# Experts begun at the last batch's gates, with u products inside a pair and D's rows split at half the pace

## The chip, the cores and the metric

The kernel runs on one core of a Trainium2 chip. Five engines work side by side, each through its own instructions in order: TensorE (PE in the profile, PEld for its weight loads), VectorE (DVE), ScalarE (ACT), GpSimd (POOL) and SyncE (SP), which here only issues DMAs. ACT issues some DMAs too. An engine that waits for a semaphore holds up everything behind it in its own order. The metric is the time of one execution in microseconds (us); lower is better. The median of three runs before the change is 789.2 us (788.12 to 789.28).

## The reference

Two mixers of the same input x (2048 rows, 640 columns) are blended by a gate per row:

```python
x = A_x
g = _sigmoid((x * gate_w).sum(-1, keepdims=True))
a = _A_ref(x, A_dft_seq_re, A_dft_seq_im, A_dft_hid_re, A_dft_hid_im)
b = _B_ref(x, B_w_q, B_k1, B_k2, B_u, B_v)
return g * a + (1 - g) * b
```

A is a Fourier mixing written as matrix products: `a = x @ dft_hid_re.T`, `b = x @ dft_hid_im.T`, and then `dft_seq_re @ a - dft_seq_im @ b`.

B is a layer of 256 tiny experts with 32 heads per row:

```python
q = jnp.einsum("nd,dhc->nhc", xf, w_q)          # 32 heads x 256 per row
s1 = jnp.einsum("nhd,ed->nhe", q[..., :dk], k1) # 16 scores
s2 = jnp.einsum("nhd,ed->nhe", q[..., dk:], k2) # 16 scores
# the two best of s1, the two best of s2, the two best of their 4 sums
# top_e: expert numbers i1 * 16 + i2 (2 per head), g: softmax of their sums
act = _gelu(jnp.einsum("nd,nhkd->nhk", xf, u[top_e]))
out = jnp.einsum("nhk,nhk,nhkd->nd", g, act, v[top_e])
```

## The kernel before

**Numbers and products.** Most matrices are held as two parts of type fp32r, a high one (`h`, made by an ACT copy, line 122) and the rest (`l`, made by a subtraction on POOL or DVE, line 123). `split` makes both; `mm3` (lines 127 to 129) multiplies them in three matmuls: high by high, high by low, low by high. Almost all of PE's work runs through `mm3`, so the profile has one line for many different products and the tiles' names tell them apart.

**The frame: 128 pieces.** The sequence transform is cut into 128 pieces n (`seq_piece`), 16 to each of eight parts q (real or imaginary matrix, four column blocks of 512). A piece is five `mm3`, 15 matmuls of 512 columns, into PSUM banks 0 to 4. A piece's tile of the matrix is loaded five pieces ahead into `wf`, and split three pieces ahead into one of four slots of `WS`. At the end of a part, ACT copies the banks out (L220), DVE multiplies them by the row gate (`gate_piece`, L192, which needs the DMA `grow`), and ACT stores them (`store_piece`). All other work is hung between the pieces: `at(n, f)` runs f behind piece n, and calls hung at one n run in the order in which they were registered. Every engine takes its instructions in the order that this yields. A tile that takes over another's buffer waits until all that read the old tile are done, those issued later among them.

**Stage 1, pieces 0 to 30.** x is loaded and split (`X`). The query weights and the keys are folded into one matrix: for each of eight groups G, at b = 6 + 3G, 32 narrow matmuls (`w_part`, L320) make a tile `wp`, which ACT copies out (L325; `wp` has one buffer, and bank 5 or 6 is freed by it). Three pieces later it is transposed in five blocks of 128: first blocks 0 to 3, then, behind the next group's `w_part`, block 4 (`w_transposes`, L331). Both go through PSUM bank 7, which ACT (L333) and DVE (L334) empty. The last group's blocks are transposed at pieces 28 and 29. Beside this run the loads and splits of u (`split_u`, pieces 24 to 28) and the first x transposed (`load_xT`, `split_xT`, piece 27).

**Stage 2, pieces 31 to 63.** Rows come in 8 pairs of 128-row tiles, four pieces to a pair. `score_half(i, a)` makes half of the scores of tile i, 15 matmuls of 512 columns into bank 5 or 6 in turn, and ACT copies them out (L424). `u_pair(p)` makes all 256 products of u for the pair, 30 matmuls of 256 columns, a gelu on ACT (L541) and two stores. A pair's order behind its four pieces is: half, half, half, then half with `u_pair`, the next pair's `split_xT` and the load of the pair after that. `xh` and `xl` have one buffer each, taken anew by every pair. On DVE `topk` picks the two best of each list, `gates` the two best sums and their softmax (per batch of four tiles), and `rows` sends expert numbers and gates through transposing DMAs (L499) into `ROWS` (ACT, L504).

**The pump.** DVE's small steps (`topk`, `gates`, `rows`, `experts`) are generators in a queue, `Pump`. Each `mm3` calls `run_bg(0.68)`, which adds `share` times 0.68 us to a credit, and while the credit is positive the next step is issued and its price taken off. Steps issued directly (`gate_piece`, `make_sums`, `split_sums`, the part sums) take their price off the same credit. `rows` is spaced out by PE time instead. `drain` issues steps without credit until a condition holds.

**Stage 3, pieces 64 to 127.** `experts` builds two one-hot matrices for each of 32 chunks on DVE (`build`, L581 to L583, price 3.3), in one of four sets of `HOT`, and two chunks on PE 16 small matmuls each (`use`, L604, into bank 5 or 6), whose result DVE reduces into `cd` (`sums`, L590 and L592, price 1.4). Chunks 0 to 15 (g = 0) need the rows of batches 0 and 1, the others those of 2 and 3. Experts begin once all rows are in place. From piece 120 on (`ending`) only sets 0 and 1 are taken, one chunk at a time; at piece 124 sets 2 and 3 (in the tile `WP`) must be free, because the last stage's ring takes their place, and `bg.drain` sees to it. Beside this, D (the hidden transform) is loaded and split (`load_dd`, `split_dd`), sums of stored parts are made (`sum_parts`, pieces 98 to 109), and sums of D's blocks (`make_sums`, `split_sums`, pieces 114 to 123; L689 to L693).

**Stage 4.** 70 steps of the hidden transform and of the expert values follow, with the same rings, and raw tiles (`take`, `give`) into which SP loads what is to be split. The rest of the chunks is pumped here too.

Of the kernel before, what the change touches and what calls it, by code (L numbers as in the profile page):

```python
# [8 lines left out]
F32 = mybir.dt.float32  # L9
# [7 lines left out]
P = 128  # L17
S = 2048
D = 640
# [71 lines left out]
def gated_mix_kernel(ctx: ExitStack, tc: tile.TileContext, xT, xn, dreT, dimT, wsre, wsim, wq, kT, uT, vv, gw, out):  # L91
# [259 lines left out]
            for n in range(2):  # L351
                nc.sync.dma_start(xf[p][:, n], xT[2 * p + n])

    def split_xT(p):
        if p < NP:
            xs[p] = tuple(big.tile([P, 2, KD, P], F32R, name=t, tag=t) for t in ("xh", "xl"))
            f = xf.pop(p)
            for n in range(2):
                split(f[:, n], xs[p][0][:, n], xs[p][1][:, n], nc.gpsimd)
            load_xT(p + 1)  # L360

    for n in range(NT - 4):
        at(n, load_x, n + 4)
# [7 lines left out]
    for G in range(NG + 1):  # L371
        b = 6 + 3 * G - 2 * (G == NG)
        if G:
            at(b, w_transposes, G - 1, 0, 4)
        if G < NG:
            for m in range(4 * G, 4 * G + 4):
                at(b, w_part, m)
            for i, m in enumerate(range(4 * G + WQB, 4 * G + WQB + 4)):
                at(b + i // 2, load_wq, m)
        if G:  # L380
            at(b + (G == NG), w_transposes, G - 1, 4, KD)
    n = b + 2
    at(n - 8, load_xT, 0)
    for k in range(KD):
        at(n - 8 + k, load_u, k)
        at(n - 6 + k, split_u, k)
    at(n - 3, split_xT, 0)
    N0 = n + 1

    def gate():  # L390
# [20 lines left out]
    picked, rowed = set(), set()  # L411

    def score_half(i, a):
        xh, xl = (t[:, i % 2] for t in xs[i // 2])
        if a == 0:
            while i > 1 and i - 2 not in picked:
                bg.one()
            scs[i] = p2.tile([P, HH, E], F32, name="sc", bufs=2)
        ps = ps_s()
        c = slice(a * TC, (a + 1) * TC)  # L420
        for k in range(KD):
            mm3(ps, xh[:, k, :], xl[:, k, :], WH[:, k, c], WL[:, k, c], k == 0, k == KD - 1)
            run_bg(0.68)
        nc.scalar.activation(scs[i].rearrange("p h e -> p (h e)")[:, c], ps, AF.Copy)  # L424
        if a == 1:
            picks(i, scs.pop(i))

    def topk(i, sc):
# [6 lines left out]
        for s in range(2):  # L435
# [10 lines left out]
            if s == 0:  # L446
# [2 lines left out]
                nc.vector.scalar_tensor_tensor(sc, eq, FAR, sc, op0=OP.mult, op1=OP.add)  # L449
                yield 1.44  # L450

    def gates(b):
        mm, rr = stats.pop(b)
        t1a, t2a = mm[:, 0, :, :H], mm[:, 0, :, H:]
        t1b, t2b = mm[:, 1, :, :H], mm[:, 1, :, H:]
        c = p2.tile([P, 3, NB, H], F32, name="cc")
        nc.vector.tensor_add(c[:, 0], t1a, t2a)
        nc.vector.tensor_add(c[:, 1], t1a, t2b)
        nc.vector.tensor_add(c[:, 2], t1b, t2a)
        pk = p2.tile([P, NB, H], F16, name="pk")  # L460
        nc.vector.tensor_tensor(pk, c[:, 1], c[:, 2], op=OP.is_ge)
        nc.vector.tensor_tensor(c[:, 1], c[:, 1], c[:, 2], op=OP.max)
        nc.vector.tensor_sub(c[:, 1], c[:, 1], c[:, 0])
        nc.scalar.activation(c[:, 2], c[:, 1], AF.Exp)
        yield 1.2
        rp = p2.tile([P, 2, NB, 2, 2, H], F16, name="rp")
        r = rp[:, :, :, 0]
        nc.vector.tensor_copy(r[:, 0, :, 0], rr[:, 0, :, :H])
        nc.vector.tensor_copy(r[:, 1, :, 0], rr[:, 0, :, H:])
        d = p2.tile([P, 2, NB, H], F16, name="dp")  # L470
        nc.vector.tensor_sub(d[:, 0], rr[:, 0, :, :H], rr[:, 1, :, :H])
        nc.vector.tensor_sub(d[:, 1], rr[:, 1, :, H:], rr[:, 0, :, H:])
        nc.vector.tensor_mul(d, d, pk[:, None].to_broadcast([P, 2, NB, H]))
        nc.vector.tensor_add(r[:, 0, :, 1], d[:, 0], rr[:, 1, :, :H])
        nc.vector.tensor_add(r[:, 1, :, 1], d[:, 1], rr[:, 0, :, H:])
        for n in range(2):
            nc.vector.tensor_copy(rp[:, n, :, 1], r[:, n])
        yield 1.3

        nc.vector.tensor_scalar(c[:, 1], c[:, 2], 1.0, None, op0=OP.add)  # L480
        nc.vector.reciprocal(c[:, 0], c[:, 1])
        nc.vector.tensor_scalar(c[:, 0], c[:, 0], GSCALE, None, op0=OP.mult)
        nc.vector.tensor_mul(c[:, 1], c[:, 0], c[:, 2])
        g = c[:, :2].rearrange("p k i h -> p i k h")
        gs = p2.tile([P, NB, 2, 2, H], F16, name="gs")
        nc.vector.tensor_copy(gs[:, :, 0], g)
        nc.vector.tensor_sub(gs[:, :, 1], g, gs[:, :, 0])
        gated[b] = (rp, gs)
        yield 1.5

    def rows(b):
        rp, gs = gated.pop(b)

        def load_rows(a):

            t = p2.tile([P, 3, P], F16, name="rt", bufs=2)
            for n in range(3):
                f = rp[:, n, a] if n < 2 else gs[:, a]
                nc.sync.dma_start(t[:, n, :], f.rearrange("p a k h -> p (a k h)"), transpose=True)  # L499
            return t  # L500

        def put_rows(a, t):
            i = b * NB + a
            nc.scalar.activation(ROWS[i // 8][:, :, :, i % 8], t, AF.Copy)  # L504
            rowed.add(i)

        got = {}

        def step(a):
            if a < NB:  # L510
                got[a] = load_rows(a)
            if a:
                put_rows(a - 1, got.pop(a - 1))

        for a in range(NB + 1):
            bg.space(lambda a=a: step(a), 5.0 if a else 16.0 if b == NT // NB - 1 else 8.0)
        yield 0.0
# [12 lines left out]
            bg.add(rows(NT // NB - 1))  # L530

    def u_pair(p):
        xh, xl = xs.pop(p)
        ps = ps_s((P, 2, 2 * P))
        for n in range(2):
            c = slice(n * P, (n + 1) * P)
            for k in range(KD):
                mm3(ps[:, n, :], UH[:, k, c], UL[:, k, c], xh[:, :, k, :], xl[:, :, k, :], k == 0, k == KD - 1)
            run_bg(1.8)
        act = p2.tile([P, 2, 2 * P], F32, name="act", bufs=2)  # L540
        nc.scalar.activation(act, ps, AF.Gelu_apprx_tanh)  # L541
        for n in range(2):
            nc.scalar.dma_start(actd[n][:, 2 * p * P:2 * (p + 1) * P], act[:, n])

    for p in range(NP):
        n = N0 + 4 * p
        for a in range(4):
            at(n + 1 + a, score_half, 2 * p + a // 2, a % 2)
        at(n + 4, u_pair, p)
        at(n + 4, split_xT, p + 1)  # L550
    N1 = N0 + 4 * NP + 1


# [12 lines left out]
    def experts():  # L566
# [7 lines left out]
        def build(g, c, s):  # L574
            pt, qt = (HOT[s // 2][:, s % 2, n].rearrange("p (m e t) -> p m e t", e=E, t=4) for n in range(2))

            def row(n):
                r = ROWS[g][:, n, 8 * c:8 * c + 8, :].rearrange("p b (s t) -> p (b s) t", t=4)
                return r[:, :, None, :].to_broadcast(shp)

            nc.vector.tensor_tensor(pt, row(0), wt, op=OP.is_equal)  # L581
            nc.vector.tensor_tensor(qt, row(1), wt, op=OP.is_equal)
            nc.vector.tensor_tensor(pt, pt, row(2), op=OP.mult)  # L583
# [28 lines left out]
        while todo or prev:  # L612
            group = []
            if todo:
                def few():
                    return len([s for s in free_sets if s < 2 or not ending]) < min(len(todo), 1 if ending else 2)
                if few():
                    yield from use(prev)
                    prev = []
                for n in range(min(len(todo), 1 if ending else 2)):  # L620
# [13 lines left out]
    def load_dd(m):  # L634

        if m < KD:
            draw[m] = big.tile([P, 2, D], F32, name="draw", tag=("xf", "xh", "xl")[m % 3])
            for a in range(2):
                w, k = divmod(2 * m + a, KD)
                nc.sync.dma_start(draw[m][:, a], (dreT, dimT)[w][k])  # L640
# [7 lines left out]
        if a == 1:  # L648
            draw.pop(m)

    for m in range(3):
        at(N1 + m, load_dd, m)
    for m in range(KD):
        for a in range(2):
            at(N1 + 3 + 2 * m + a, split_dd, m, a)
        at(N1 + 4 + 2 * m, load_dd, m + 3)

# [66 lines left out]
    at(NPC + 28, store_gates, 1)  # L726


    raw_free, raw_tags = deque(), [("wf", 1)] * 5 + [(f"X{s}", 2) for s in range(10, 16)] + [("xf", 2)]
    raw, sp = {}, {}  # L730

    def take(key):
        if raw_tags:
            t, n = raw_tags.pop(0)
            if t == "wf":
                raw_free.append(big.tile([P, TC], F32, name="ra", tag=t, bufs=5))
            else:
                r = big.tile([P, 2, TC], F32, name="ra", tag=t)
                raw_free.extend(r[:, a] for a in range(2))
        raw[key] = f = raw_free.popleft()  # L740
        return f

    def give(key):
# [245 lines left out]
    prep_split = {NPC - 4: (0,), NPC - 3: (1,), NPC - 2: (2,), NPC - 1: (3, 4)}  # L989
    WP = None  # L990
    for n in range(N0, NPC):
        ending = n >= NPC - 8
        share = 0.95 if p3 is None or ending else 1.05
        seq_piece(n)
        follow(n)
        if n >= N1 and p3 is None and len(rowed) == NT and n % NT not in (NT - 2, NT - 1):
            p2_stack.close()
            p3 = ctx.enter_context(tc.tile_pool(name="p3", bufs=1, reuse_waits="tile"))
            pools.append(p3)
            HOT.append(p3.tile([P, 2, 2, 16 * E * 4], F16, name="hot0"))  # L1000
            HOT.append(p3.tile([P, 2, 2, 16 * E * 4], F16, name="hot1", tag="WP"))
            bg.add(experts(), late=True)
        if n == NPC - 4:
            bg.drain(lambda: {2, 3} <= set(free_sets))
            HOT.pop()
# [56 lines left out]
```

## Time and profile before

| what | value |
|---|---|
| median of three runs | 789.2 us |
| the profiled execution | 790.35 us, its span 788.5 us |
| PE busy | 772.8 us, 98% of the span |
| DVE busy | 553.7 us, 70% |
| POOL, ACT busy | 336.2 us (43%), 275.0 us (35%) |
| mean granted TensorE clock | 0.994 |
| pieces 15, 31, 47, 63 end near | 68, 142, 263, 386 us (first L220) |
| pieces 79, 95, 111, 127 end near | 447, 505, 562, 628 us |

The span runs from the first to the last instruction; the execution's time has what lies around it as well. A name like "PE b L129" is the engine, the tile that is written and the line. Where PE is busy at a granted clock of 1.00, another engine's idle time costs nothing. A wait is put down to the instruction that released it. In the timeline a row's figures are its start, its length, and in brackets the idle time of its engine before it, with the releaser.

### The profile page before, as it was taken

The numbers are of one execution on the slowest core, as the hardware profiler recorded it, in microseconds if no ns is written. First come the engines' busy times: TensorE is split into PE (matmuls) and PEld (weight loads), VectorE is DVE, ScalarE is ACT, GpSimd is POOL, SyncE is SP. The second block draws the span as 40 slices with busy tenths as digits, with TensorE's granted clock in tenths as the row PEclk, the third lists the DMA queues.
The fourth block names the chain that finished last, engine by engine and source line by source line (L and its number), as shares of the span: only waits on it lengthen the run. The fifth ranks groups of instructions, "written<-read, shape, count | busy, mean of one in ns | idle before, by whom it ended". The sixth has DMA issues, their size and how long they took to land.

```text
span 788.5 us, 10998 instructions
## 1 busy us (share of the span) xinstructions
PE 772.8 (98%) x4116; PEld 626.0 (79%) x4116; DVE 553.7 (70%) x660; ACT 275.0 (35%) x445; POOL 336.2 (43%) x233
## 2 busy tenths in 40 slices
PE   8999999999999999999999999999999899999997
PEld 6777767887888888878888888888888688888886
DVE  5741042287898999999895178799799948836651
ACT  4434223322323523523533711311324353334350
POOL 5423324314424233144149643353456473468270
PEclk9999999999999999999999999999999899999999
DMA  9876893502112242130355342568744695559421
GB/s 339 328 293 193 339 336 131 200 6 95 45 56 86 63 154 81 52 123 29 96 187 169 119 147 73 170 212 283 259 175 161 206 303 199 141 176 306 130 82 67
DMA packets 75508, 130.31 MB, mean 165 GB/s; under 512 B 17088, under 2 KB 24128, under 8 KB 75200
## 3 DMA queue, kind: packets, MB, share of 16 engines
q1 hardware_dynamic: 62704, 112.18, 42.8%
q10 hardware_dynamic: 12752, 17.45, 6.0%
q8 instruction: 32, 0.52, 0.3%
q14 instruction: 20, 0.16, 0.1%
HBM read 102.84 MB, written 25.17 MB: 162 GB/s over the span
## 4 chain that ended last, share of the span: by engine, by line
PE 76%; issue 9%; DVE 8%; DMA 3%; POOL 2%; SPq 1%; ACT 0%; DVEq 0%; ACTq 0%; POOLq 0%
PE b L127 24%; PE b L129 24%; PE b L128 24%; PE b L320 2%; POOL xl L123 2%; DMA xr<-in_xn 1%; PE b L604 1%; DVE hot L583 1%; DMA gd<-cd 1%; DMA pd<-ST 1%; DVE tmp L590 1%; DMA wf<-in_wsre 1%; DVE tf L691 1%; PE b L331 1%; DVE tf L692 1%
## 5 line engine op out<-in xcount | busy, mean ns | idle before, releaser
L123 POOL TENSOR_TENSOR WS<-wf,WS 128x512 fp32r<-128x512 f32 x127 | 190.6, 1506 | 283.4 <-ACT WS L122 283.3
L127 PE MATMUL b<-WS,X 128*128 128x512 f32 x635 | 251.3, 396 | 0.0
L128 PE MATMUL b<-WS,X 128*128 128x512 f32 x635 | 248.9, 392 | 0.7 <-POOL WS L123 0.7
L129 PE MATMUL b<-WS,X 128*128 128x512 f32 x635 | 248.7, 392 | 0.0
L128 PEld LDWEIGHTS b<-WS,X 128*128 128x128 f32 x635 | 120.3, 189 | 25.7 <-POOL WS L123 1.5
L127 PEld LDWEIGHTS b<-WS,X 128*128 128x128 f32 x635 | 120.5, 190 | 25.4 <-issue 0.5
L129 PEld LDWEIGHTS b<-WS,X 128*128 128x128 f32 x635 | 120.0, 189 | 25.3
L122 ACT ACTIVATE WS<-wf 128x512 fp32r<-128x512 f32 x128 | 79.7, 627 | 156.8 <-PE b L129 87.9
L129 PE MATMUL b<-WU,xl 128*128 128x512 f32 x160 | 63.1, 394 | 2.2 <-POOL xl L123 1.7
L123 POOL TENSOR_TENSOR xl<-xf,xh 128x640 fp32r<-128x640 f32 x16 | 32.1, 2031 | 73.9 <-ACT xh L122 73.9
L127 PE MATMUL b<-WU,xh 128*128 128x512 f32 x160 | 62.3, 390 | 0.0
L128 PE MATMUL b<-WU,xh 128*128 128x512 f32 x160 | 62.3, 389 | 0.0
L424 ACT ACTIVATE sc<-b 128x512 f32<-128x512 f32 x32 | 20.2, 630 | 114.3 <-PE b L129 114.3
L123 POOL TENSOR_TENSOR WS<-ra,WS 128x512 fp32r<-128x512 f32 x32 | 46.4, 1472 | 28.8 <-ACT WS L122 27.3
L192 DVE SCALAR_TENSOR_TENSOR ST<-ST,grow 128x512 f32<-128x512 f32 x40 | 34.6, 928 | 31.3 <-DMA grow<-gdr 31.3
L438 DVE TENSOR_REDUCE mm<-sc 128x64 f32<-128x1024 f32 x32 | 38.9, 1216 | 25.0 <-ACT sc L424 24.5
L334 DVE TENSOR_TENSOR WU<-b,WU 128x512 fp32r<-128x512 f32 (+1 forms) x16 | 7.9, 491 | 59.5 <-ACT WU L333 59.5
L440 DVE TENSOR_TENSOR eq<-sc,mm 128x1024 f16<-128x1024 f32 x32 | 43.4, 1356 | 1.1
L123 POOL TENSOR_TENSOR WP<-ra,WP 128x512 fp32r<-128x512 f32 x18 | 28.4, 1587 | 33.8 <-ACT WP L122 33.6
L590 DVE TENSOR_TENSOR tmp<-b,mask 128x512 f32<-128x512 f32 x32 | 22.0, 688 | 25.4 <-PE b L604 24.5
L444 DVE TENSOR_REDUCE rr<-eq 128x64 f16<-128x1024 f16 x32 | 39.0, 1220 | 1.1
L129 PEld LDWEIGHTS b<-WU,xl 128*128 128x128 f32 x160 | 30.0, 188 | 11.2 <-POOL xl L123 5.1
(148 smaller groups left out, 1248.1 us busy)
## 6 DMA issues: line engine op xcount, KB each, us to landing
wq<-in_wq SPq DMA_DIRECT2D x32, 640.0 KB, 6.7
wf<-in_wsre SPq DMA_DIRECT2D x64, 256.0 KB, 5.2
wf<-in_wsim SPq DMA_DIRECT2D x64, 256.0 KB, 3.8
ra<-pd SPq DMA_DIRECT2D x50, 256.0 KB, 3.6
pd<-ST ACTq DMA_DIRECT2D x40, 256.0 KB, 3.9
xr<-in_xn SPq DMA_DIRECT2D x16, 320.0 KB, 5.9
xf<-in_xT SPq DMA_DIRECT2D x16, 320.0 KB, 3.3
ra<-pqs SPq DMA_DIRECT2D x20, 256.0 KB, 4.7
```

The lines of the kernel that those rows point to most:

```text
L122: nc.scalar.activation(h, f, AF.Copy)
L123: eng.tensor_sub(l, f, h.bitcast(F32))
L127: nc.tensor.matmul(o, wh, ah, start=first, stop=False, skip_group_check=more)
L128: nc.tensor.matmul(o, wh, al, start=False, stop=False, skip_group_check=more)
L129: nc.tensor.matmul(o, wl, ah, start=False, stop=last, skip_group_check=more)
L192: nc.vector.scalar_tensor_tensor(f, f, -1.0 if w else 1.0, g, op0=OP.mult, op1=OP.mult)
L320: nc.tensor.matmul(ps[32 * j:32 * j + 32, :HALF], kp[:, 8 * G // H, r, :], w[:, j], start=(r == 0), stop=(r == 1))
L424: nc.scalar.activation(scs[i].rearrange("p h e -> p (h e)")[:, c], ps, AF.Copy)
L438: nc.vector.tensor_reduce(m, sc, op=OP.max, axis=AX.X)
L440: nc.vector.tensor_tensor(eq, sc, m[:, :, None].to_broadcast([P, HH, E]), op=OP.is_equal)
L444: nc.vector.tensor_reduce(r, eq, op=OP.max, axis=AX.X)
L590: nc.vector.tensor_tensor(tmp, t.rearrange("p m (e t) -> p (m e) t", t=4), mask4[:, None, :].to_broadcast([P, 8 * E, 4]), op=OP.mult)
```

## The change

Five things are changed.

1. In stage 1 block 4 of each group is transposed one piece later than before, at b + 1 (the last group's stays where it was).
2. In stage 2 `xh` and `xl` are one tile each for the whole stage, and each half of a pair is split by a call of its own: `u_pair` stands ahead of the third score half, the next pair's first half is split right behind it, and the second half behind the fourth score half. The load of the pair after that is issued two pieces later.
3. `experts` are added as soon as the last batch's gates are made, with 10.0 taken from the credit. The last batch's rows and gates live in a tile of their own (`lb`, in the place of `xl`), so that the memory of stage 2 can be given up before the rows are sent. `share` stays 0.95 throughout. `ending` starts at piece 117, and while it lasts, chunks in sets 2 and 3 are used before another is built.
4. D's ten rows are split every second piece instead of every piece, through two buffers instead of three.
5. `take` hands out raw tiles that were never used before it hands out returned ones.

```diff
-    def split_xT(p):
+    def split_xT(p, n):
         if p < NP:
-            xs[p] = tuple(big.tile([P, 2, KD, P], F32R, name=t, tag=t) for t in ("xh", "xl"))
-            f = xf.pop(p)
-            for n in range(2):
-                split(f[:, n], xs[p][0][:, n], xs[p][1][:, n], nc.gpsimd)
-            load_xT(p + 1)
+            if not xs:
+                xs.update((t, big.tile([P, 2, KD, P], F32R, name=t, tag=t)) for t in ("xh", "xl"))
+            split(xf[p][:, n], xs["xh"][:, n], xs["xl"][:, n], nc.gpsimd)
...
-            at(b + (G == NG), w_transposes, G - 1, 4, KD)
+            at(b + 1, w_transposes, G - 1, 4, KD)
...
-    at(n - 3, split_xT, 0)
+    for a in range(2):
+        at(n - 3, split_xT, 0, a)
+    at(n - 2, load_xT, 1)
...
-        rp = p2.tile([P, 2, NB, 2, 2, H], F16, name="rp")
+        if b == NT // NB - 1:
+            f = last_rows()
+            rp = f[:, :8 * P].rearrange("p (n i a k h) -> p n i a k h", n=2, i=NB, a=2, k=2)
+            gs = f[:, 8 * P:12 * P].rearrange("p (i a k h) -> p i a k h", i=NB, a=2, k=2)
+        else:
+            rp = p2.tile([P, 2, NB, 2, 2, H], F16, name="rp")
+            gs = p2.tile([P, NB, 2, 2, H], F16, name="gs")
...
     for p in range(NP):
         n = N0 + 4 * p
         for a in range(4):
+            if a == 2:
+                at(n + 3, u_pair, p)
+                at(n + 3, split_xT, p + 1, 0)
             at(n + 1 + a, score_half, 2 * p + a // 2, a % 2)
-        at(n + 4, u_pair, p)
-        at(n + 4, split_xT, p + 1)
+        at(n + 4, split_xT, p + 1, 1)
+        at(n + 6, load_xT, p + 2)
...
-                if few():
+                if few() or ending and any(s > 1 for g, c, s in prev):
                     yield from use(prev)
                     prev = []
...
-            draw[m] = big.tile([P, 2, D], F32, name="draw", tag=("xf", "xh", "xl")[m % 3])
+            draw[m] = big.tile([P, 2, D], F32, name="draw", tag=("xf", "xh")[m % 2])
...
-            at(N1 + 3 + 2 * m + a, split_dd, m, a)
-        at(N1 + 4 + 2 * m, load_dd, m + 3)
+            at(N1 + 3 + 4 * m + 2 * a, split_dd, m, a)
+        at(N1 + 7 + 4 * m, load_dd, m + 2)
...
-        if raw_tags:
+        if not fresh and raw_tags:
             t, n = raw_tags.pop(0)
             if t == "wf":
-                raw_free.append(big.tile([P, TC], F32, name="ra", tag=t, bufs=5))
+                fresh.append(big.tile([P, TC], F32, name="ra", tag=t, bufs=5))
             else:
                 r = big.tile([P, 2, TC], F32, name="ra", tag=t)
-                raw_free.extend(r[:, a] for a in range(2))
-        raw[key] = f = raw_free.popleft()
+                fresh.extend(r[:, a] for a in range(2))
+        raw[key] = f = (fresh or raw_free).popleft()
...
-        ending = n >= NPC - 8
-        share = 0.95 if p3 is None or ending else 1.05
+        ending = n >= NPC - 11
         seq_piece(n)
         follow(n)
-        if n >= N1 and p3 is None and len(rowed) == NT and n % NT not in (NT - 2, NT - 1):
+        if n >= N1 and p3 is None and NT // NB - 1 in gated:
             p2_stack.close()
...
             bg.add(experts(), late=True)
+            bg.credit -= 10.0
```

More of the change, by code (lines that the diff above doesn't have):

```diff
@@ L413, in score_half @@
     def score_half(i, a):
-        xh, xl = (t[:, i % 2] for t in xs[i // 2])
+        xh, xl = (xs[t][:, i % 2] for t in ("xh", "xl"))
         if a == 0:
@@ L450, in topk, with last_rows @@
                 yield 1.44
+    LB = []
+    def last_rows():
+        if not LB:
+            LB.append(big.tile([P, 18 * P], F16, name="lb", tag="xl"))
+        return LB[0]
     def gates(b):
@@ L484, in gates @@
         g = c[:, :2].rearrange("p k i h -> p i k h")
-        gs = p2.tile([P, NB, 2, 2, H], F16, name="gs")
         nc.vector.tensor_copy(gs[:, :, 0], g)
@@ L491, in rows @@
     def rows(b):
-        rp, gs = gated.pop(b)
+        rp, gs = gated[b]
         def load_rows(a):
-            t = p2.tile([P, 3, P], F16, name="rt", bufs=2)
+            if b == NT // NB - 1:
+                t = last_rows()[:, (12 + 3 * (a % 2)) * P:][:, :3 * P].rearrange("p (n m) -> p n m", n=3)
+            else:
+                t = p2.tile([P, 3, P], F16, name="rt", bufs=2)
             for n in range(3):
@@ L532, in u_pair @@
     def u_pair(p):
-        xh, xl = xs.pop(p)
+        xh, xl = xs["xh"], xs["xl"]
         ps = ps_s((P, 2, 2 * P))
@@ L579, in row @@
                 return r[:, :, None, :].to_broadcast(shp)
+            assert rowed >= set(range(8 * g, 8 * g + 8))
             nc.vector.tensor_tensor(pt, row(0), wt, op=OP.is_equal)
@@ L649, in split_dd @@
             draw.pop(m)
-    for m in range(3):
+    for m in range(2):
         at(N1 + m, load_dd, m)
@@ L726, in gated_mix_kernel @@
     at(NPC + 28, store_gates, 1)
-    raw_free, raw_tags = deque(), [("wf", 1)] * 5 + [(f"X{s}", 2) for s in range(10, 16)] + [("xf", 2)]
+    fresh, raw_free, raw_tags = deque(), deque(), [("wf", 1)] * 5 + [(f"X{s}", 2) for s in range(10, 16)] + [("xf", 2)]
     raw, sp = {}, {}
     def take(key):
-        if raw_tags:
+        if not fresh and raw_tags:
             t, n = raw_tags.pop(0)
             if t == "wf":
-                raw_free.append(big.tile([P, TC], F32, name="ra", tag=t, bufs=5))
+                fresh.append(big.tile([P, TC], F32, name="ra", tag=t, bufs=5))
             else:
                 r = big.tile([P, 2, TC], F32, name="ra", tag=t)
-                raw_free.extend(r[:, a] for a in range(2))
-        raw[key] = f = raw_free.popleft()
+                fresh.extend(r[:, a] for a in range(2))
+        raw[key] = f = (fresh or raw_free).popleft()
         return f
```

## The prediction

> **What bounds the kernel now.** The table of engines comes first:
>
> ```profile
> PE 772.8 (98%) x4116; PEld 626.0 (79%) x4116; DVE 553.7 (70%) x660; ACT 275.0 (35%) x445; POOL 336.2 (43%) x233
> ```
>
> TensorE is the bound, and the change takes no matmul away. Time can only come from moments in which PE stands still or runs at a lower granted clock. The windows show where (busy time per engine, mean granted clock, DMA share, GB/s):
>
> ```profile
> 108.00:124.00 16.00, 14.16 (x81) 10.35 (x80) 4.02 (x5) 3.70 (x10) 3.86 (x3) 0.89 0.93 329
> 124.00:138.00 14.00, 14.00 (x89) 10.49 (x88) 3.55 (x5) 5.66 (x12) 6.71 (x5) 1.00 0.20 63
> 424.00:450.00 26.00, 26.00 (x116) 21.52 (x116) 0.29 (x1) 15.18 (x19) 19.60 (x15) 1.00 0.44 139
> 540.00:600.00 60.00, 60.00 (x357) 49.07 (x352) 54.14 (x74) 17.26 (x34) 28.15 (x21) 1.00 0.64 220
> 600.00:626.00 26.00, 22.09 (x147) 17.43 (x147) 24.64 (x37) 8.46 (x19) 15.87 (x12) 0.87 0.52 166
> ```
>
> The table of waits (total, times, longest) names what ended the holes:
>
> ```profile
> ACT wp L325 <- PE b L331: 13.5, 7, 2.2
> PEld b L129 <- POOL xl L123: 5.1, 7, 1.3
> PE b L604 <- DVE tmp L590: 3.9, 2, 3.0
> PE b L331 <- DVE WU L334: 3.2, 3, 1.8
> ```
>
> Three kinds of hole, then: the fifth transpose of a W group waits for the split of the first four (L331), a score half waits for the low part of x (xl), and expert products wait for the sums of earlier ones (L604). Here they are in the timeline, the idle time in brackets:
>
> ```profile
> 46.10 0.33 PE L331 MATMUL b<-identf,wp 128*128 128x128 f32 x1 [0.22 <-DVE WU L334]
> 60.55 0.33 PE L331 MATMUL b<-identf,wp 128*128 128x128 f32 x1 [1.13 <-DVE WU L334]
> 115.35 0.33 PE L331 MATMUL b<-identf,wp 128*128 128x128 f32 x1 [1.84 <-DVE WU L334]
> 335.61 0.39 PE L127 MATMUL b<-WU,xh 128*128 128x512 f32 x1
> 335.83 0.39 PE L128 MATMUL b<-WU,xh 128*128 128x512 f32 x1
> 337.14 0.50 PE L129 MATMUL b<-WU,xl 128*128 128x512 f32 x1 [0.92 <-POOL xl L123]
> 610.16 0.69 PE L604 MATMUL b<-hot 128*64 128x64 f16 x32
> 615.47 0.64 PE L604 MATMUL b<-hot 128*64 128x64 f16 x16 [3.02 <-DVE tmp L590]
> 616.99 0.64 PE L604 MATMUL b<-hot 128*64 128x64 f16 x16 [0.88 <-DVE tmp L590]
> ```
>
> **Part 1, the fifth transpose one piece later (+4.95, then -5.5).** For groups G = 0 to 6 it used to follow the 32 products of W at piece b; now it follows piece b+1. Its wait for L334 then lies behind 15 matmuls, some 3.4 us at the 0.22 to 0.23 us between starts above, so the idle 0.22 + 1.13 + 1.84 = 3.19 us goes. The window 108:124 ran at a mean clock of 0.89, although 124:138 with the same kind of work ran at 1.00: 0.11 x 16 = 1.76 us, which I put down to the idle time at 115 just before. Gain 4.95 us.
>
> The same edit moves a second wait. ACT copies each new wp (L325) into the one buffer that the fifth transpose of the group before still reads; the 13.5 us in seven waits above are that. Now ACT stands at L325 for a whole piece more, and behind it in ACT's order wait the splits of the pieces (L122). For the copies of groups 1 to 6 there is room: the split held up is for piece b+4, two pieces or 6.8 us after ACT goes on. For those of group 7 (b = 27) there is none. The fifth transpose of group 6 and the four of group 7 both fall behind piece 28, back to back. The four need PSUM bank 7 (so L333 and L334 of the fifth) and the new wp (so L325). ACT's order from the release on is in the timeline of before:
>
> ```profile
> 130.22 0.33 PE L331 MATMUL b<-identf,wp 128*128 128x128 f32 x1
> 130.65 0.77 ACT L325 ACTIVATE wp<-b 128x320 f32<-128x320 f32 x2 [2.01 <-PE b L331]
> 131.30 0.28 ACT L333 ACTIVATE WU<-b 128x128 fp32r<-128x128 f32 x1
> 131.46 0.43 ACT L122 ACTIVATE WU<-uf 128x256 fp32r<-128x256 f32 x1
> 131.76 1.37 ACT L122 ACTIVATE xh<-xf 128x640 fp32r<-128x640 f32 x2
> 133.02 0.64 ACT L122 ACTIVATE WS<-wf 128x512 fp32r<-128x512 f32 x1
> 134.46 0.60 ACT L333 ACTIVATE WU<-b 128x512 fp32r<-128x512 f32 x1 [0.81 <-PE b L331]
> 131.62 0.29 DVE L334 TENSOR_TENSOR WU<-b,WU 128x128 fp32r<-128x128 f32 x1 [2.26 <-ACT WU L333]
> ```
>
> After the change L333 of the fifth comes behind the WS copy: 0.43 from transpose to L325, then 0.65, 0.30, 1.26 and 0.54 (its 0.64 less the 0.1 by which such rows overlap) from start to start, 3.2 us; 0.32 more to L334, 0.29 of its own, and PE goes on 3.8 us after the transpose instead of 0.1: a new hole of 3.7 us where before there was none. Bounds: 1.3 us if only L325 and L334 counted, 3.8 if everything does. After an idle 1.84 us the clock cost 1.76; I take as much here (bounds 0 and twice that, 3.5). Loss 5.5 us. Part 1 nets about -0.5.
>
> **Part 2, scores (+4.1).** Until now both halves of xh and xl were made after the u products, with one piece (3.4 us) to cover ACT and POOL. Now the u products come before the third score half, the first half is split right behind them and the second behind the fourth score half; each has two pieces and two score halves, some 13 us, before it is read. The row for 337.14 starts 1.31 us after its neighbour instead of 0.22. Over the seven such places the excess of start-to-start time, with the 0.11 of the matmul after, is 0.67 + 0.67 + 0.41 + 0.37 + 0.41 + 1.19 + 0.37 = 4.1 us, between PE's own idle and the 5.1 us that the weight loads waited. The counts stay: per pair 30 u matmuls, one gelu, two stores on ACT, two splits. The next pair's two loads move past two pieces' wf loads on SP, and still have a piece, a score half and the u products before their split. ACT waits behind the gelu as before. Nothing in this order is late next, unless xf itself is; I count 0 for that.
>
> **Part 3, experts from the last gates (+6.2).** The planner credits 5 x 0.68 us per piece. A chunk costs 3.3 + 1.4 = 4.7. Before, experts were added at piece 80 and earned 3.57 a piece (share 1.05); by my count of credits 24 chunks were built when the last stage's rule began at piece 120. At piece 124 chunks 22 and 23 (sets 2 and 3) were built and not multiplied, so the drain there forced four products with one after another's sums behind make_sums on DVE: the hole at 612. Now they are added at piece 69 or 70, pay 10.0 first, and earn 3.23. First build at piece 73, and between 73 and 116 there are 44 x 3.23 = 142, less 11.25 for three gate pieces, 15 for the part sums, 6 and 1 for two sums and a split: 109, or 23 chunks. From 117 on only one chunk at a time is begun, and a pair in sets 2 and 3 is used before anything is built. Pieces 117 to 121 earn 16, less 6 + 3, enough for the build under way and then that use at piece 122. The drain at 124 finds nothing to do.
>
> What goes is the idle 3.02 + 0.88, and the lower clock behind it: 0.13 x 26 = 3.4 us by the window's 0.87, of which the share 22.09/26 in which PE ran is 2.8. Together 6.7. In its place chunks 24 and 25 are multiplied at piece 124 and need the banks of 22 and 23, whose sums stand ahead of the last make_sums, but behind the one before. I charge 0.5 (bounds 0 and the old 3.9).
>
> What the early start costs lies under this:
>
> ```profile
> 422.89 1.41 DVE L487 TENSOR_TENSOR gs<-cc,gs 128x256 f16<-128x256 f32 x1
> 450.63 4.20 DVE L192 SCALAR_TENSOR_TENSOR ST<-ST,grow 128x512 f32<-128x512 f32 x5 [26.33 <-DMA grow<-gdr]
> L581 DVE TENSOR_TENSOR hot<-rows,wtab x32: 675/683/1773, 454.9 to 683.1; 128x1024 f16<-128x1024 f16 x32
> L582 DVE TENSOR_TENSOR hot<-rows,wtab x32: 675/684/1782, 456.4 to 683.9; 128x1024 f16<-128x1024 f16 x32
> ```
>
> DVE stood idle for 26 us there. A build of three such operations takes 2.0 to 5.3 us; some nine fit before piece 85, so 18 to 48 us on a free engine. The grow load for piece 80 may hold DVE a few us; no product waits for it before piece 84. Batch 3's rows now wait for the repaid credit, and end at piece 84 instead of 80; the first group that needs them is built from 96.
>
> **Part 4, D's rows at half the pace, two buffers; raw tiles (0).** Ten splits stay ten, on ACT and POOL. They moved no matmul before and are needed only at piece 128, 40 pieces on. POOL, 19.60 of 26 us busy in that window, gets room. Loads stay ten, each behind a release two pieces old. The raw tiles change only which buffer SP fills; PE had no hole after 626, so a gain there is hidden, and a late load would have to lose five steps first.
>
> **Sum.** 4.95 - 5.5 + 4.1 + 6.2 = 9.75 us, from a profiled time of 790.35 (its span 788.5 and 1.85 around it), which lies 1.15 above the median 789.2 of the runs. By the median: **779.5 us**.
>
> **Rivals.**
> *The stop at piece 28 costs nothing*: 779.5 - 5.5 = 774.0. It needs the framework to tie L325 to something earlier than the fifth transpose. Against it, L325 waited for L331 seven times.
> *The drain stays*: DVE or the credits are later than my count and sets 2 and 3 are still in use at 124. Then 789.2 + 0.5 - 4.1 = 785.6. For it: DVE is 54.14 of 60 us busy ahead of that place.
> *The half clock at 116 isn't the idle time's doing*: W's narrow products and the transposes, which stay, cause it. Then part 1 gains 3.2 and the time is 781.3. Against it: other groups with the same products kept 1.00, as 124:138 shows. [...]
> *Slower: builds too dear beside POOL.* If each build took 5.3 us as in the longest rows, a chunk with its sums would take DVE 6.7 us against the 4.95 us of PE time (4.7/0.95) at which chunks are issued: 1.75 behind per chunk. With 11 us of lead between build and product, PE pays from the seventh chunk; if it lasts for the first 16, 28 - 11 = 17 us, and 779.5 + 17 = 796.5. It decides once the operations average over 1.2 us. For it: POOL's D splits now run beside the first builds. Against it: medians of 0.68. [...]
>
> **How the numbers follow.** Forecast 0.55; stop free 0.12; drain stays 0.12; clock stays 0.08; slower 0.08; nothing of it arrives (789) 0.05. A difference under 0.2% (1.6 us) can't be told from none. Faster takes the first four, less a little of the drain case: 0.85; same 0.07; slower 0.08. The forecast's own range is 776 to 784 (hole at 28 from 1.3 to 7.2 with its clock, 0 to 3.9 at 124). To leave out no more than 2 in 10, I go up to the drain case and take in the lower edge: 775 to 786.5.
>
> **What would show it.** Right: no idle before the fifth transposes; one new PE idle of some 3.7 us before an L331 group near 129 to 133 us, released by DVE L334, with a granted clock under 1 behind it; no PE wait for xl; DVE building hot from about 420; no PE wait for tmp near 600 to 617, and the clock at 1.00 there. Wrong: PE waiting for hot or tmp between 430 and 600, for WS after a W group, or an L604 wait at 612 as before.

## The result and the profile after

The changed kernel takes 782.58 us (median of six, 782.25 to 783.25), the kernel before 788.14 us beside it (six, 786.66 to 789.28). The ratio is 0.993 (95% interval 0.9918 to 0.9943): 5.6 us faster. The direction and the range held; the forecast of 779.5 was 3.1 us too low, and 9.7 us of gain were promised, of which 5.6 came. One execution of the kernel before, beside e9 to e11, took 851.05 us at a granted clock of 0.851 instead of 0.994 to 0.998, and no comparison rests on it.

The profiled execution of after took 782.4 us. Its page, table of engines:

```profile
span 780.6 us, 11020 instructions
PE 769.4 (99%) x4116; PEld 624.5 (80%) x4116; DVE 564.5 (72%) x660; ACT 274.0 (35%) x445; POOL 333.7 (43%) x233
```

The same matmuls, and an end 7.9 us earlier than in the profile of before (that one was among the longer executions of its kernel, as will be seen). The windows of after, columns as before:

```profile
108.00:124.00 16.00, 16.00 (x105) 11.71 (x107) 5.63 (x9) 4.82 (x11) 4.82 (x4) 1.00 0.89 306
124.00:139.00 15.00, 11.52 (x64) 8.56 (x57) 2.80 (x6) 5.02 (x12) 5.71 (x4) 0.89 0.35 109
424.00:450.00 26.00, 26.00 (x173) 21.14 (x172) 23.21 (x23) 10.49 (x16) 16.07 (x11) 1.00 0.42 131
600.00:626.00 26.00, 26.00 (x186) 20.91 (x185) 23.14 (x34) 12.10 (x23) 14.25 (x12) 1.00 0.69 217
635.00:640.00 5.00, 4.08 (x17) 2.82 (x16) 0.00 (x0) 4.53 (x10) 4.51 (x4) 1.00 1.05 403
640.00:645.00 5.00, 4.39 (x34) 3.03 (x32) 0.00 (x0) 1.70 (x4) 5.00 (x5) 1.00 1.04 391
```

The holes at 108 to 124 and 600 to 626 us are gone, and the DVE's idle time from 424 to 450 is filled with builds. A new hole stands at 124 to 139, with a granted clock of 0.89 (0.50 from 133 to 135 us). Two small ones at 635 to 645 had not been foreseen. The timeline of after has the three, and for the first ACT's and DVE's rows as well:

```profile
129.02 0.27 PE L331 MATMUL b<-identf,wp 128*128 128x128 f32 x1
129.38 0.77 ACT L325 ACTIVATE wp<-b 128x320 f32<-128x320 f32 x2 [5.49 <-PE b L331]
132.11 0.27 ACT L333 ACTIVATE WU<-b 128x128 fp32r<-128x128 f32 x1
132.42 0.29 DVE L334 TENSOR_TENSOR WU<-b,WU 128x128 fp32r<-128x128 f32 x1 [1.51 <-ACT WU L333]
132.77 1.11 PE L331 MATMUL b<-identf,wp 128*128 128x128 f32 x4 [3.48 <-DVE WU L334]
636.81 0.50 PE L128 MATMUL b<-WP,DD 128*128 128x512 f32 x1 [0.85 <-POOL WP L123]
641.82 0.50 PE L128 MATMUL b<-WS,DD 128*128 128x512 f32 x1 [0.61 <-POOL WS L123]
```

### The profile page after: what moved, and what is told of

It is laid out like the page before. It is cut to its first block, busy times and chain, and to the rows that moved or that the text cites. A ratio compares the mean times of both kernels' runs of the same rounds, so it can differ in the third digit from the quotient of the medians.

```text
span 780.6 us, 11020 instructions
## 1 busy us (share of the span) xinstructions
PE 769.4 (99%) x4116; PEld 624.5 (80%) x4116; DVE 564.5 (72%) x660; ACT 274.0 (35%) x445; POOL 333.7 (43%) x233
## 4 chain that ended last, share of the span: by engine, by line
PE 88%; DVE 4%; issue 3%; POOL 3%; DMA 1%; ACT 0%; SPq 0%; DVEq 0%; POOLq 0%; ACTq 0%
PE b L127 28%; PE b L128 28%; PE b L129 28%; PE b L320 2%; POOL WS L123 1%; PE b L625 1%; POOL WP L123 1%; DMA wf<-in_wsre 1%; PE b L331 1%; DVE tf L710 1%; DVE tf L713 1%; DVE ts L123 0%; DVE tmp L611 0%; DVE tf L711 0%; DVE hot L604 0%
## 5 line engine op out<-in xcount | busy, mean ns | idle before, releaser
L123 POOL TENSOR_TENSOR xl<-xf,xh 128x640 fp32r<-128x640 f32 x16 | 27.1, 1694 | 84.6 <-ACT xh L122 84.6
L441 DVE TENSOR_TENSOR eq<-sc,mm 128x1024 f16<-128x1024 f32 x32 | 49.9, 1559 | 1.1
L334 DVE TENSOR_TENSOR WU<-b,WU 128x512 fp32r<-128x512 f32 (+1 forms) x16 | 7.8, 490 | 50.8 <-ACT WU L333 50.8
L192 DVE SCALAR_TENSOR_TENSOR ST<-ST,grow 128x512 f32<-128x512 f32 x40 | 37.0, 987 | 4.1 <-ACT ST L220 4.1
L122 ACT ACTIVATE WS<-ra 128x512 fp32r<-128x512 f32 x46 | 28.3, 630 | 28.0 <-PE b L129 16.7
```

What stands on the lines that cost most here:

```text
L122: nc.scalar.activation(h, f, AF.Copy)
L123: eng.tensor_sub(l, f, h.bitcast(F32))
L192: nc.vector.scalar_tensor_tensor(f, f, -1.0 if w else 1.0, g, op0=OP.mult, op1=OP.mult)
L441: nc.vector.tensor_tensor(eq, sc, m[:, :, None].to_broadcast([P, HH, E]), op=OP.is_equal)
```

## The experiments

In what follows, e2, e5 and so on are changed kernels built one on the other; "before" is timed anew beside each of three groups, e1 to e4, e5 to e8 and e9 to e11. Its medians were 787.85, 788.79 and 788.47 us, which is why small differences are taken between kernels of one group where possible.

**The order of raw tiles.** My first suspicion for the holes at 636 and 641 us fell on part 5: a load into `xf` that now comes two tiles earlier. In e1 the old order is restored:

```diff
-        if not fresh and raw_tags:
+        if raw_tags:
...
-        raw[key] = f = (fresh or raw_free).popleft()
+        raw[key] = f = raw_free.popleft()
```

> The changed kernel with one part undone: raw tiles are handed out in the old order. Theory: the third s1 load (now into xf, 9 us behind the second, its wait ended by DVE) bunches the loads and stores that follow, and PE then waits at 636.8 and 641.8 us; in the old order xf comes two tiles later, so both waits go, with an excess of 0.23 + 1.12 + 0.77 = 2.1 us between matmul starts: about 780.5 by the scale of 782.6, a ratio to the kernel before of 0.990. Rival: ACT's five stores of the last part (3.7 us of issue) make the holes whatever the tiles; then 782.6, 0.993, and a PE wait for WP near 636 stays.

782.32 us (780.86 to 783.8), and both waits stand where they were:

```profile
635.33 0.50 PE L128 MATMUL b<-WP,DD 128*128 128x512 f32 x1 [0.85 <-POOL WP L123]
640.33 0.50 PE L128 MATMUL b<-WS,DD 128*128 128x512 f32 x1 [0.58 <-POOL WS L123]
```

The suspicion fell. The order of raw tiles moves nothing that can be measured, here and in e3 below, which came out at e2's time and not at the 775.5 us that I expected.

**The stop at piece 28.** e2 puts group 6's block 4 back to piece 27 and leaves the other six a piece later; e3 adds the old order of raw tiles.

```diff
-            at(b + 1, w_transposes, G - 1, 4, KD)
+            at(b + (G != NG - 1), w_transposes, G - 1, 4, KD)
```

> The changed kernel, except that block 4 of group 6 is transposed at piece 27 as before; the others stay one piece later. Theory: the hole of 3.48 us at 132.8 goes, and with it the window of 3.4 us at half clock, 1.5 us beyond the idle time: 782.6 - 5.0 = 777.6, a ratio of about 0.987, mean clock 1.00 in the whole span but for its ends. Rival 1: the low clock is a matter of the narrow products and the transposes and stays: 779.1. Rival 2: the wait moves to the next transposes at piece 28: no gain.

> The two edits together (old order of raw tiles; group 6's block 4 at piece 27). Theory: places 500 us apart, so the gains add: 782.6 - 2.1 - 5.0 = 775.5, a ratio of 0.984. Rival: the last stage starts 5 us earlier in absolute time but at the same distance from its own loads, yet DMA at over 0.95 of its time from 635 to 650 us sets a floor, and part of it is given back: 777 to 778.

e2 took 777.11 us (776.99 to 777.29), e3 776.99. The window of e2 is full and at full clock:

```profile
124.00:139.00 15.00, 15.00 (x87) 11.65 (x78) 4.62 (x7) 7.43 (x16) 9.62 (x7) 1.00 0.53 180
```

One transpose went one piece back, and the kernel is 5.5 us faster than after, 5.2 faster than e1, which has the same first stage and was timed in e2's own group. The prediction's term for the stop was 5.5. The scatter fell as well, from 1.0 us to 0.3.

**The fifth transposes by themselves.** e4 is the kernel before with this part alone, all seven moved; e11 the kernel before with the six that do no harm.

```diff
-            at(b + (G == NG), w_transposes, G - 1, 4, KD)
+            at(b + 1, w_transposes, G - 1, 4, KD)              # e4
+            at(b + (G != NG - 1), w_transposes, G - 1, 4, KD)  # e11
```

> The kernel before with the fifth transposes alone moved by one piece. Theory: 3.2 us of idle time before them and the half clock behind the one at 115 go, a hole of 3.5 us with its own half clock comes at piece 28: no change within 1 us (the first stage's end moves by less than 1 us). Rival: the hole at 28 needs another part of the change (the split of x in halves lies in the same place of ACT's order); then 3.2 to 4.9 us faster.

> The kernel before with only the fifth transposes of groups 0 to 5 moved by one piece, those of groups 6 and 7 where they were. Theory: 3.2 us of idle time go without a new hole, and the half clock at 116 us with them wherever an execution had it: 3.2 to 4.9 us faster than before, 783.5 to 785.5. Rival: the half clock isn't the idle time's doing; then 3.2 at most, and a window of half clock stays near 113 to 120 us in the trace.

e4: 790.06 us, a ratio of 1.0027 (1.0011 to 1.0042), slower than before by 2.2 us, where I had expected no change within 1 us. e11: 785.4 us, 0.9962 (0.9947 to 0.9977), faster by 3.1 (1.8 to 4.2 by the interval). In e11's trace the window 108 to 124 us has PE busy for all of 16.00 us at a clock of 1.00, with every product and transpose still there:

```profile
108.00:124.00 16.00, 16.00 (x108) 11.68 (x111) 5.64 (x9) 4.83 (x11) 4.67 (x4) 1.00 0.90 303
```

So moving six transposes is worth their idle time of 3.2 us and little more, and moving the seventh costs 5.2 to 5.5. Why the half clock (0.50 from 117 to 120 us in the profile of before) adds so little to the first sum is told below.

**The holes at 636 and 641 us.** The timelines of before, of after and of e5 show where ACT and DVE differ behind the end of piece 127, whose first L220 starts at 628.01, 617.76 and 612.61 us. Before (DVE, then ACT):

```profile
628.95 0.69 DVE L583 TENSOR_TENSOR hot<-hot,rows 128x1024 f16<-128x1024 f16 x1
629.55 3.10 DVE L192 SCALAR_TENSOR_TENSOR ST<-ST,grow 128x512 f32<-128x512 f32 x5
636.44 0.42 ACT L715 ACTIVATE ts<-vxl 128x256 fp32r<-128x256 f32 x1 [1.94 <-DVE vxl L123]
641.44 0.63 ACT L122 ACTIVATE WP<-ra 128x512 fp32r<-128x512 f32 x1 [4.05 <-DMA pd<-ST]
```

After, where L736 is the old L715:

```profile
619.50 0.69 DVE L611 TENSOR_TENSOR tmp<-b,mask 128x512 f32<-128x512 f32 x1 [2.37 <-PE b L625]
622.03 0.68 DVE L604 TENSOR_TENSOR hot<-hot,rows 128x1024 f16<-128x1024 f16 x1
622.64 6.38 DVE L192 SCALAR_TENSOR_TENSOR ST<-ST,grow 128x512 f32<-128x512 f32 x5
628.94 1.48 DVE L123 TENSOR_TENSOR vxl<-dt,vxh 128x1280 fp32r<-128x1280 f32 x1
630.45 0.42 ACT L736 ACTIVATE ts<-vxl 128x256 fp32r<-128x256 f32 x1 [5.60 <-DVE vxl L123]
634.78 0.63 ACT L122 ACTIVATE WP<-ra 128x512 fp32r<-128x512 f32 x1 [3.39 <-DMA pd<-ST]
622.28 4.99 POOL L123 TENSOR_TENSOR WS<-ra,WS 128x512 fp32r<-128x512 f32 x3 [8.11 <-DMA ra<-gd]
```

The last row is POOL's. The pump's credits now happen to put a chunk's sums and another's build behind piece 127, ahead of the last `gate_piece` in DVE's order. The gates start 4.9 us behind the L220 instead of 1.5, fall beside POOL's splits, and take 6.38 us instead of 3.10. The low part of v comes after them, ACT stands 5.6 us for it, then 3.4 more in its stores, and the split of WP that PE needs is late. e5 is e2 with no credit given during piece 127:

```diff
         ending = n >= NPC - 11
+        share = 0.0 if n == NPC - 1 else 0.95
```

> e2 with no credit given during piece 127, so that the chunk multiplied, summed and built there moves behind piece 128's row gates on DVE. Theory: that chunk stands in front of the last gate_piece (its sums wait 2.4 us for PE, three builds 1.9 us), pushes the five L192 under POOL's splits (6.4 us instead of 3.1), and so the low part of v, ACT's copy of it, and the split of WP behind it; with it gone PE's two waits at 631.6 and 636.6 us (excess 1.14 + 0.74 + 0.29) go: 777.1 - 2.1 = 775.0. Rival: ACT's stores into a DMA queue that is busy over 95% hold ACT for 3.8 us anyway, and at least the second wait stays: 776.5 to 777.1.

774.49 us (774.31 to 774.72), 2.6 less than e2 (2.5 less than e6 below, which takes e2's time and was timed in e5's group), a ratio to before of 0.9821 (0.9803 to 0.984). PE waits nowhere in the last stage, although ACT stands as long in its stores as in after, 3.42 us against 3.39; the stores alone, the rival of e1 and e5, do not make the holes:

```profile
613.24 3.41 DVE L192 SCALAR_TENSOR_TENSOR ST<-ST,grow 128x512 f32<-128x512 f32 x5 [1.28 <-ACT ST L220]
620.47 0.42 ACT L736 ACTIVATE ts<-vxl 128x256 fp32r<-128x256 f32 x1 [1.37 <-DVE vxl L123]
624.83 0.63 ACT L122 ACTIVATE WP<-ra 128x512 fp32r<-128x512 f32 x1 [3.42 <-DMA pd<-ST]
```

This beats both kernels of the case, by 8.1 and by some 14 us.

**The parts of the expert change.** e6 is e2 with the old end rule, e7 e2 with the late start (all rows in place, nothing held back, share 0.95, the new end rule kept).

```diff
-        ending = n >= NPC - 11                                            # e6
+        ending = n >= NPC - 8
-                if few() or ending and any(s > 1 for g, c, s in prev):
+                if few():
...
-        if n >= N1 and p3 is None and NT // NB - 1 in gated:              # e7
+        if n >= N1 and p3 is None and len(rowed) == NT and n % NT not in (NT - 2, NT - 1):
...
-            bg.credit -= 10.0
```

> e2 without the new end rule: single chunks only from piece 120, and no use of a pair ahead of building. Theory: by the count of credits chunks 22 and 23 are multiplied at piece 122 with or without it, the drain at 124 finds nothing, and the time is the same: 777.1 within 0.4. Rival: the end rule is what empties sets 2 and 3; then products wait for sums near 600 us for some 4 us, with half clock in part of the runs: 781 to 784.

> e2 with the late start: experts are added when all rows are in place (piece 80 or 81), nothing held back, share 0.95. 18 instead of 22 chunks would be done by piece 117 by the count of credits, and the end rule still empties sets 2 and 3 by piece 122. Theory: the end rule suffices, no wait near 600 us; thirteen instead of six chunks fall to the last stage, where DVE has room: 776 to 778. Rival: the early start is what pays; with it gone DVE is late before 600 or in the last stage, and PE waits: 780 or more.

e6: 776.97 us, the same as e2's 777.11. The early start empties the sets in time without the new end rule, which does nothing here. e7: 789.84 us, the rival's forecast and not mine. PE waits 1.4 us for a build near 610 us and 1.0 us for a sum near 618, but most of the backlog went on to the next forced drain, in the middle of the last stage, where all that is left is issued at once. The timeline of e7:

```profile
697.76 0.44 PE L625 MATMUL b<-hot 128*64 128x64 f16 x16
699.97 0.44 PE L625 MATMUL b<-hot 128*64 128x64 f16 x16 [1.76 <-DVE tmp L611]
704.07 0.64 PE L625 MATMUL b<-hot 128*64 128x64 f16 x16 [3.66 <-DVE tmp L611]
```

and the window around it, with its clock of 0.83:

```profile
690.00:710.00 20.00, 14.58 (x110) 11.54 (x110) 16.50 (x21) 4.18 (x7) 7.93 (x6) 0.83 0.23 69
```

With the lower share but without the early start the kernel is as slow as before. e7 does not tell how a late start does at the old share of 1.05.

**The credit held back.** e10 is e5 without it.

```diff
-            bg.credit -= 10.0
```

> e5 without the 10.0 held back at the start. By the count of credits the first build moves from piece 73 to 70 and the lead at piece 117 grows by two chunks. Theory: PE was nowhere waiting for the experts any more, so nothing is gained: 774.5 within 0.4. Rival: builds now start in the middle of the gates' own slow steps and of D's splits (DVE was 98% busy from 414 to 424 us), and products wait; 776 or more.

778.63 us, 4.1 more than e5: the rival was right. The first products now wait for their builds:

```profile
417.94 1.77 DVE L603 TENSOR_TENSOR hot<-rows,wtab 128x1024 f16<-128x1024 f16 x1
419.64 2.06 DVE L604 TENSOR_TENSOR hot<-hot,rows 128x1024 f16<-128x1024 f16 x1
421.62 1.75 DVE L602 TENSOR_TENSOR hot<-rows,wtab 128x1024 f16<-128x1024 f16 x1
424.63 0.44 PE L625 MATMUL b<-hot 128*64 128x64 f16 x16 [2.43 <-DVE hot L604]
```

The credits issue a build as if DVE were up to date; it still has the gates' slow steps in front of it and takes up to 2.06 us for an operation beside POOL. In the profiled execution the waits, 2.7 us together, were followed by a lower clock as well, 0.83 on the mean of 420 to 430 us; the execution with a clock of 1.000 took 777.52 us.

**The score stage, D's pace.** e8 is e2 with the old order of the score stage, one split for both halves behind the u products at the end of a pair; e9 is e5 with D's rows split every piece.

```diff
-            if a == 2:                                            # e8
-                at(n + 3, u_pair, p)
-                at(n + 3, split_xT, p + 1, 0)
...
-            at(N1 + 3 + 4 * m + 2 * a, split_dd, m, a)            # e9
-        at(N1 + 7 + 4 * m, load_dd, m + 2)
+            at(N1 + 3 + 2 * m + a, split_dd, m, a)
+        at(N1 + 5 + 2 * m, load_dd, m + 2)
```

> e2 with the order of the score stage as before (both halves split behind the u products at the end of a pair). Theory: the seven waits for xl come back, 4.1 us of excess between starts: 777.1 + 4.1 = 781.2. Rival: with the credit at other points the DVE's lead differs and part is taken back in stage 3 (a later experts' start leaves more to the end): 779 to 780.

> e5 with D's ten rows split every piece again (through two buffers). Theory: their pace costs or saves nothing that PE sees, 774.5 within 0.4; in the trace the first builds beside POOL's splits are longer, and no product waits for them. Rival: with both dense between 407 and 440 us the DVE falls behind the pace at which chunks are issued, and products wait for hot or tmp before 480 us: 776 or more.

e8: 780.88 us (780.85 to 781.15), 3.8 more than e2, and the seven waits for xl are back in its trace:

```profile
PEld b L129 <- POOL xl L123: 5.2, 7, 1.4
```

e9: 774.44 us, as e5. The operations of its first six builds are longer, with medians near 1.78 us beside POOL's denser splits, and no product waits for them. D's pace is free either way.

## Why the prediction was right or wrong

**Right in place.** Every hole that was to go went, and the one that was to come came where it was put and by the chain it was given, with L333 behind ACT's splits and L334 last: 3.48 us of idle time against 3.7. With its clock it costs 5.2 to 5.5 us against 5.5 (e2). Part of that agreement is luck: the hole without half clock costs some 3.8 us (e1's 780.86 us at a clock of 1.000, against e2), and the rest depends on how often the half clock comes. The score stage gave 3.8 us for 4.1 (e8). Part 4 was worth nothing (e9, e1). The rivals "the stop at piece 28 costs nothing" and "the drain stays" fell with the trace of after. The rival that the half clock at 116 isn't the idle time's doing has every trace against it: in those of all twelve changed kernels the window at 108 to 124 us, without the idle time and with the same products, ran at 1.00, against 0.89 in before. (Its sum of 781.3 took away the first hole's 1.76 us of clock and kept the new hole's; without both it would have been the forecast again.)

**The term that was too large: 4.95 us for the fifth transposes.** The chip gave 3.1 (e11), and 4.95 lies outside e11's interval. The step that failed is "0.11 x 16 = 1.76 us, which I put down to the idle time at 115": right of the profiled execution, wrong as a price. The prediction took the half clock for something that every execution pays, and the runs don't bear that out. The two low windows of the profile of before, 0.89 over 16 us and 0.87 over 26 us, account for its mean clock of 0.994 ((1.76 + 3.38) of 788.5 us). Of the 37 other executions of before in the three groups 7 have 0.994, with a median of 789.8 us; 17 have 0.996 (788.3) and 13 have 0.998 (787.4), so that in most of them a part of these stretches is missing. The profile, at 790.35 us, was slower than all six of the timed ones, by 2.2 us than their median. That it is the stretch at 115 us that is often missing is inferred: no second trace has this idle time. The longer new hole shows it directly: e1 has the same 3.48 us of idle time in its profile, without a half clock behind it, and took 780.86 us, while its other executions reach 783.8 at a mean clock of 0.995. Part 1 nets not -0.5 but about -2.2 (e4).

**The term that was missing: 2.6 us in the last stage.** The prediction counted the credits up to piece 124, where the drain looks, and stopped there. The count itself held as far as it went: the drain left PE no wait, with or without the end rule (e6), and the waits for tmp near 600 us are gone. But the same count, carried on by three pieces, puts a chunk in front of the last row gates. "A late load would have to lose five steps first" was right of loads, and beside the point: what came late was DVE's part of v (e5).

**The 0.5 us for products at piece 124** was not needed; PE has no wait there. From the start of piece 111's copies to those of 127 after needs 57.0 us (560.8 to 617.8) and before 65.0 (563.0 to 628.0), 8.0 more, of which about 1 is three chunks' products that now lie elsewhere. That agrees with the 6.7 us for the old hole. (Of these, 2.8 are for the clock, taken from one profile like the 1.76; the window's own figures give 2.9, and in the trace of e4 the clock there is 0.93 instead of 0.87.) The runs agree: e9 lies 11.0 us below e11 in one group, and without the 3.8 of the score order some 7 us are left for the experts' start with the credit of piece 127 withheld.

**The slower rival** was right as a mechanism and held off by the 10.0 of credit: builds beside POOL do take 1.8 to 2.1 us an operation, and without the credit PE waits for them (e10). Between 423 and 447 us in the trace of after each of the eight build operations of 1.78 to 2.06 us starts while one of POOL's splits runs; those that start while POOL stands idle take 0.68 to 0.69. In e9 the operations of the first six builds take 1.61 us on the mean, above the 1.2 at which the prediction had the rival decided, and PE waits for none of them; by the prediction's sum the lead was to last for just six chunks.

Together: 9.7 - 1.9 for the fifth transposes - 2.6 for the last stage + 0.2 for the two smaller terms = 5.4, against 5.6 measured. Two things let the forecast look better than its parts. The base of 789.2 us, a median of three, was 1.1 us above the 788.1 of the six, so that the time is off by 3.1 us where the gain is off by 4.1. And the range held although the loss in the last stage stood among none of its bounds.

## What to carry to other kernels

When an instruction is moved behind a point that an in-order engine waits for, follow that engine's queue past the wait, and look at the last turn of the loop by itself: six turns gained 3 us and the seventh lost over 5. Where background work is paced by credits, carry the count past the place that is being mended, to the next point where the same engine owes something; a chunk in front of the wrong instruction cost 2.6 us, and a late start moved most of the forced work to a later drain. And before a stall's aftermath is priced from one profile, see whether the other executions have it: a profile slower than the timed runs shows a price that is not always paid.

## What had not been expected

The half clock behind a short idle time differs from one execution to the next. Idle 1.84 us at 115 us was followed by it in the profile of before; idle 3.48 us was in the profiles of after and e4 (0.89 in the same window) and was not in that of e1, where the window is otherwise the same:

```profile
124.00:139.00 15.00, 11.52 (x73) 8.49 (x63) 3.35 (x6) 5.22 (x12) 6.76 (x5) 1.00 0.34 118
```

Kernels without such holes also scatter less, for the most part: e2 0.3 us, e5 0.4, e8 0.3, against 1.0 for after, 2.9 for e1 and 5.6 for e4. The clock isn't all of it: one execution of e9 took 1.5 us more than its other three at a clock of 1.000, and two of before took 789.8 us at 0.998. What decides whether the half clock comes, no run here shows.
